# Retention attention with a gated feed-forward on one core: separate attention steps in place of a three-chunk group, and a first part shared out otherwise

## The chip, the core and the metric

The kernel runs on one NeuronCore of a Trainium2 chip. The core has five engines that work side by side, each through its own queue and in order: PE (TensorE, matrix multiplication; its weight loads are listed as PEld), DVE (VectorE), ACT (ScalarE), POOL (GpSimd) and SP (SyncE, which here only issues DMAs). Matrix products go from SBUF to PSUM[...]. The metric is the time of one execution on the device in microseconds (us), less is better.

## The reference

There are q, k and v of shape 8 x 8 x 576 x 64 (batch, heads, sequence, head dimension), all float32. The reference computes retention, which is attention without a softmax, and then a feed-forward layer:

```python
scores = scale * np.matmul(q, k.transpose(0, 1, 3, 2))
Dmat = np.where(rel >= 0, gamma[:, None, None] ** rel[None, :, :], 0.0)   # rel = row - column
attn_out = np.matmul(scores * Dmat, v)
x = attn_out.transpose(0, 2, 1, 3).reshape(B * S, H * D)                  # 4608 x 512
h = x @ w_in                                                            # 4608 x 2048
out = (h * (1.0 / (1.0 + np.exp(-beta * h)))) @ w_out                    # 4608 x 512
```

Each head has its own decay gamma, and beta has a value for each of the 2048 hidden columns.

## The kernel before

**Attention.** A batch's 576 positions are cut into four chunks of 128 and one of 64, so there are 40 chunks, numbered from 0 in order of batch and position; chunks 4, 9, 14 and so on have 64 rows. The decay is taken apart: q is multiplied by a power of gamma that depends on its position, v by the inverse power. So inside a chunk only a causal mask is left, and what earlier chunks contribute is a running sum of k times v, the state. For chunk i there are these steps, whose names are used throughout:

- `pre`: scale and cast q to `qn`, cast k to `kn`, scale and cast v to `vn`. For chunks 0 to 3 this is shared by DVE (qn), ACT (kn) and POOL (vn), later all is POOL's.
- `load_next`: issue the loads of q, k, v seven chunks ahead (`NQ`) on SP.
- `a_T`: eight PE transposes of qn and kn into one PSUM tile `T`, then one ACT copy of it to `qkT` (L193, L197).
- `a_sc`: eight score matmuls. A head has 64 dimensions, so each uses 64 of the 128 array rows (L209). DVE then multiplies by the mask, twice, to give `R` (L213).
- `a_O`: eight matmuls of R with vn (L224). Each takes 64 columns of vn, the two heads of a pair going to the lower and upper 64 partitions of `O`. If the chunk is not the batch's first, four matmuls of q with the state `sbd` are added (L228). DVE copies O to `xT` (L231), the transposed input of the feed-forward layer.
- `a_st`: four matmuls that add the chunk to the state (L243), and two ACT copies to `sbd` (L249). It is left out for a batch's last chunk.

**Feed-forward.** The 4608 tokens are cut into nine blocks of 512. A block m has 16 `up` steps (four matmuls of 512 columns and a Silu on ACT, L261 and L263), then 16 `down` steps (four matmuls each, L273); after every fourth, DVE copies the result to `ot` and SP stores it (L279, L281). Weights are loaded in four pieces each, and cast by DVE and POOL (`cast_w_in`, L124; `cast_w_out`, L136, which divides by beta).

**Order.** The order is written out by hand. `merged` walks through a list of up and down steps, here called fills, and puts attention steps between them at given positions. Until chunk 3 attention runs alone, with matmuls on zeros (`warm_up`, L146) in the gaps. Chunks 4 to 8 are placed as separate steps: `attn_steps(i, at)` puts `pre` four fills ahead, a_T at `at`, a_sc two fills later, a_st and a_O two fills after that. From chunk 9 on `cluster(i, at)` puts three steps of successive chunks in one place:

```python
st += [(at - 4, F(pre, i)), (at - 3.9, F(load_next, i)), (at, F(a_T, i))]
st += [(at, F(a_sc, i - 1))]
st += [(at, F(a_O, i - 2)), (at, F(a_st, i - 2))]
```

The lines are those of the kernel before.

Of the kernel before, what the change touches and what calls it, by code (L numbers as in the profile page):

```python
# [19 lines left out]
def kernel(  # L20
# [10 lines left out]
    nc = tc.nc  # L31
# [51 lines left out]
    for h in range(H):  # L83
# [12 lines left out]
                            fill=0.0, base=0, channel_multiplier=-1)  # L96

    NS = 2
    sbds = [consts.tile([P, HP, P], BF16, name=f"sbd{i}") for i in range(NS)]
    nc.vector.memset(sbds[0][:], 0.0)  # L100
    nc.vector.memset(sbds[1][:], 0.0)

# [6 lines left out]
    WG = 4  # L109
    FG = d_ff // WG  # L110
    w_in_r = moe_w_in.rearrange("(ko ki) f -> ki ko f", ki=P)
    w_out_r = moe_w_out.rearrange("(fo fi) n -> fi fo n", fi=P)
    wts = {}

    def load_w_in(g):
        t = stage.tile([P, KO, FG], F32, name="wt", tag="wt", bufs=4)
        nc.sync.dma_start(t[:], w_in_r[:, :, g * FG:(g + 1) * FG])
        wts[g] = t

    def cast_w_in(g):  # L120
        t = wts.pop(g)
        for ko in range(KO):
            e = nc.gpsimd if ko == KO - 1 else nc.vector
            e.tensor_copy(w_in_sb[:, ko, g * FG:(g + 1) * FG], t[:, ko])  # L124

    def load_w_out(g):
        t = stage.tile([P, KO, d_model], F32, name="wt", tag="wt", bufs=4)
        nc.sync.dma_start(t[:], w_out_r[:, g * KO:(g + 1) * KO, :])
        wts[WG + g] = t

    def cast_w_out(g):
        t = wts.pop(WG + g)
        for i in range(KO):
            fo = g * KO + i
            e = nc.gpsimd if i == KO - 1 else nc.vector
            e.tensor_scalar(w_out_sb[:, fo, :], t[:, i], rbeta_sb[:, fo:fo + 1], None, ALU.mult)  # L136

    for g in range(WG):
        load_w_in(g)
# [8 lines left out]
    def betas():  # L148
        pb = psum.tile([P, FO], F32, name="pb", tag="T", bufs=1)
        nc.tensor.transpose(pb[:], beta_rows[:], ident_f[:FO, :FO])  # L150

        nc.vector.tensor_copy(beta_sb[:], pb[:])
        nc.vector.tensor_tensor(tiny[:], beta_sb[:], beta_sb[:], ALU.mult)  # L153
        nc.vector.tensor_scalar(tiny[:], tiny[:], 1e-24, 1e-12, ALU.is_lt, ALU.mult)
        nc.vector.tensor_tensor(beta_sb[:], beta_sb[:], tiny[:], ALU.add)
        nc.vector.reciprocal(rbeta_sb[:], beta_sb[:])
# [6 lines left out]
    def pre(i):  # L163
# [5 lines left out]
        qn = sb.tile([P, H, D], BF16, name="qn", tag="qn", bufs=3)  # L169
        kn = sb.tile([P, H, D], BF16, name="kn", tag="kn", bufs=4)  # L170
        vn = sb.tile([P, H, D], BF16, name="vn", tag="vn", bufs=4)
        gq_b = gq[:cL, c, :].unsqueeze(2).to_broadcast([cL, H, D])
        gv_b = gv[:cL, c, :].unsqueeze(2).to_broadcast([cL, H, D])
        (nc.vector if first else nc.gpsimd).tensor_tensor(qn[:cL], t[:cL, 0], gq_b, ALU.mult)  # L174
        if first:
            nc.scalar.copy(kn[:cL], t[:cL, 1])
        else:
            nc.gpsimd.tensor_copy(kn[:cL], t[:cL, 1])  # L178
        nc.gpsimd.tensor_tensor(vn[:cL], t[:cL, 2], gv_b, ALU.mult)  # L179
        live[i] = dict(qn=qn, kn=kn, vn=vn)  # L180

# [4 lines left out]
    def a_T(i):  # L186
# [3 lines left out]
        T = psum.tile([P, 2, HP, P], BF16, name="T", tag="T", bufs=1)  # L190
        for j, src in enumerate((L["qn"], L["kn"])):
            for p in range(HP):
                nc.tensor.transpose(T[:, j, p, :cL],  # L193
                                    src[:cL, 2 * p:2 * p + 2, :].rearrange("p h d -> p (h d)"),
                                    ident[:cL, :cL])
        qkT = sb.tile([P, 2, HP, P], BF16, name="qkT", tag="qkT", bufs=4)
        nc.scalar.copy(qkT[:, :, :, :cL], T[:, :, :, :cL])  # L197
        L["qT"], L["kT"] = qkT[:, 0], qkT[:, 1]
# [17 lines left out]
    def a_O(i):  # L216
        b, c = order[i]
        c0, cL = chunks[c]
        L = live[i]
        R, vn = L["R"], L["vn"]  # L220
        O = psum.tile([P, HP, P], F32, name="O", tag="O", bufs=1)
        for p in range(HP):
            for j in range(2):
                nc.tensor.matmul(O[j * D:(j + 1) * D, p, :cL], vn[:cL, 2 * p + j, :], R[:cL, j, p, :cL],  # L224
                                 start=(p == 0), stop=(c == 0), skip_group_check=True)
        if c > 0:
            for p in range(HP):
                nc.tensor.matmul(O[:, p, :cL], sbds[(i - 1) % NS][:, p, :], L["qT"][:, p, :cL],  # L228
                                 start=False, stop=True, skip_group_check=True)
        n0 = b * S + c0  # L230
        nc.vector.tensor_copy(xT[:, :, n0:n0 + cL], O[:, :, :cL])  # L231

    def a_st(i):
# [8 lines left out]
        for p in range(HP):  # L242
            nc.tensor.matmul(st[:, p, :], L["kn"][:cL, 2 * p:2 * p + 2, :].rearrange("p h d -> p (h d)"),  # L243
                             L["vn"][:cL, 2 * p:2 * p + 2, :].rearrange("p h d -> p (h d)"), start=(c == 0 and p == 0), stop=True,
                             skip_group_check=True)
# [55 lines left out]

    warm_up(12)
    betas()
    pre(0)
    a_T(0)
    pre(1)
    for i in range(4):
        warm_up(2)
        a_sc(i)
        a_st(i)  # L310
        if i < 3:
            a_T(i + 1)
            if i < 2:
                pre(i + 2)
        else:
            cast_w_in(0)
            warm_up(2)
        a_O(i)

    fill = [F(up, 0, fo) for fo in range(FO)]  # L320
    merged(fill, [(2, F(cast_w_in, 1)), (5, F(cast_w_in, 2)), (9, F(cast_w_in, 3))],
           [(5.1 + g / 10, F(load_w_out, g)) for g in range(2)],
# [3 lines left out]
    for i in range(5):  # L326
# [18 lines left out]
                                          if b * S + chunks[c][0] + chunks[c][1] >= (m + 1) * MB), len(order)))  # L345

    C0 = done
    clusters = []

    def cluster(i, at):  # L350
        last = len(order) - 1
        st = []
        if i <= last:
            st += [(at - 4, F(pre, i)), (at - 3.9, F(load_next, i)), (at, F(a_T, i))]
        if C0 <= i - 1 <= last:
            st += [(at, F(a_sc, i - 1))]
        if C0 <= i - 2 <= last:
            st += [(at, F(a_O, i - 2)), (at, F(a_st, i - 2))]
        return st

    for m in range(1, NMB - 1):
        base = n1 if m == 1 else len(fill)
        if m > 1:
            fill += [F(up, m, fo) for fo in range(FO)]
            fill += [F(down, m, ms, f0) for ms in range(MB // P) for f0 in range(0, FO, 4)]
        todo = list(range(done, need(m + 1) + 2))
        streams += [cluster(i, base + n * 31 / len(todo)) for n, i in enumerate(todo)]
        done = need(m + 1) + 2
    for m in range(NMB - 1, NMB):
        fill += [F(up, m, fo) for fo in range(FO)]  # L370
        fill += [F(down, m, ms, f0) for ms in range(MB // P) for f0 in range(0, FO, 4)]
    merged(fill, *streams)

# [29 lines left out]
```

## Time and profile before

| | |
|---|---|
| median of three runs | 333.45 us (333.25 to 335.33) |
| the profiled execution | 333.45 us |
| its span, first to last instruction | 331.7 us |
| mean granted TensorE clock | 0.994 |
| PE busy | 318.0 us, 96% of the span |
| ACT, DVE, POOL busy | 165.5, 111.3, 110.3 us |
| read from HBM, written | 36.71 MB, 9.44 MB |

The span is what the profile sees; the time has some 1.75 us more around it. A line of a timeline gives start, duration, engine, source line, operation, output and inputs, shape and count, and in brackets how long the engine was idle before and for whom. Matmuls overlap in the pipeline, so the durations shown for them add up to more than the time that passes: it is the starts that tell the pitch. Some matmul records are missing, so that 7 or 31 stand where 8 or 32 ran.

### The profile page before, as it was taken

How to read it: one execution, taken by the hardware profiler on the slowest of the kernel's cores; microseconds unless marked ns; L12 is line 12 of the kernel's file. 1: busy time of each engine (PE TensorE's matmuls, PEld its weight loads, DVE VectorE, ACT ScalarE, POOL GpSimd, SP SyncE). 2: the span in 40 equal slices, each digit the busy share in tenths (PEclk: the TensorE clock that was granted, in tenths of full speed). 3: DMA queues.
4: the chain of work that ended last, by engine and by line, in shares of the span. 5: the costliest groups of instructions: out<-in, count | busy, mean ns of one | idle time of the engine just before them, and what ended most of it. 6: DMA issues, size and time to landing. Idle time of an engine off the chain costs nothing.

```text
span 331.7 us, 5914 instructions
## 1 busy us (share of the span) xinstructions
PE 318.0 (96%) x2415; PEld 169.1 (51%) x2455; DVE 111.3 (34%) x202; ACT 165.5 (50%) x272; POOL 110.3 (33%) x129
## 2 busy tenths in 40 slices
PE   6779899999999999999999999999999999999995
PEld 2544584576555555555555554555554555444442
DVE  3774372624531244123331232123333332220011
ACT  2667781295337722871188226822784257405700
POOL 2224757975443333322335333323335200000000
PEclk9799999999999999999999999999999999999999
DMA  9999999999999988904692169313000110011011
GB/s 171 220 383 226 268 375 219 209 211 234 243 189 271 209 151 199 196 1 104 154 239 62 40 158 239 74 35 110 34 1 2 63 65 0 2 68 58 2 63 63
DMA packets 121979, 46.53 MB, mean 140 GB/s; under 512 B 113232, under 2 KB 113248, under 8 KB 121952
## 3 DMA queue, kind: packets, MB, share of 16 engines
q1 hardware_dynamic: 121920, 46.15, 62.4%
q8 instruction: 19, 0.31, 0.4%
q14 instruction: 8, 0.07, 0.1%
q10 hardware_dynamic: 32, 0.01, 0.0%
HBM read 36.71 MB, written 9.44 MB: 139 GB/s over the span
## 4 chain that ended last, share of the span: by engine, by line
PE 94%; DVE 3%; issue 1%; ACT 0%
PE ph L261 38%; PE po L273 37%; PE T L193 5%; PE O L224 4%; PE sc L209 4%; PE O L228 3%; PE st L243 2%; PE ph L146 2%; DVE R L213 2%; DVE xT L231 0%; ACT qkT L197 0%; DVE w_in_sb L124 0%; DVE tiny L153 0%; DVE ot L279 0%; DVE qn L174 0%
## 5 line engine op out<-in xcount | busy, mean ns | idle before, releaser
L261 PE MATMUL ph<-xT,w_in_sb 128*128 128x512 bf16 (+2 forms) x622 | 126.9, 357 | 2.2 <-DVE xT L231 1.1
L273 PE MATMUL po<-w_out_sb,gT 128*128 128x512 bf16 x556 | 125.7, 379 | 1.1
L263 ACT ACTIVATE gT<-ph,beta_sb 128x512 bf16<-128x512 f32 (+2 forms) x160 | 102.0, 645 | 39.1 <-PE ph L261 37.9
L261 PEld LDWEIGHTS <-w_in_sb 128*128 128x128 bf16 x640 | 60.5, 98 | 60.0 <-issue 1.6
L273 PEld LDWEIGHTS <-gT 128*128 128x128 bf16 x576 | 55.3, 98 | 63.2
L213 DVE TENSOR_TENSOR R<-sc,causal 128x512 bf16<-128x512 f32 (+1 forms) x80 | 47.2, 631 | 114.6 <-PE sc L209 114.2
L197 ACT COPY qkT<-T 128x1024 bf16<-128x1024 bf16 (+1 forms) x40 | 37.0, 924 | 90.8 <-PE T L193 90.7
L179 POOL TENSOR_TENSOR vn<-qkvn,gv 128x512 bf16<-128x512 f32 (+1 forms) x40 | 41.6, 1040 | 65.9 <-PE st L243 26.7
L279 DVE COPY ot<-po 128x512 f32<-128x512 f32 x36 | 24.8, 691 | 85.4 <-PE po L273 85.4
L178 POOL CAST kn<-qkvn 128x512 bf16<-128x512 f32 (+1 forms) x36 | 21.9, 608 | 70.6 <-PE st L243 53.0
L174 POOL TENSOR_TENSOR qn<-qkvn,gq 128x512 bf16<-128x512 f32 (+1 forms) x36 | 37.6, 1045 | 2.9 <-DMA qkvn<-in_q_dram 2.4
L249 ACT CAST sbd<-st 64x256 bf16<-64x256 f32 x64 | 23.4, 366 | 15.8 <-PE st L243 14.7
L231 DVE CAST xT<-O 128x512 bf16<-128x512 f32 (+1 forms) x40 | 25.3, 632 | 6.0 <-PE O L228 5.5
L224 PE MATMUL O<-R,vn 128*64 128x128 bf16 (+1 forms) x320 | 16.9, 221 | 2.0 <-DVE R L213 2.0
L193 PE MATMUL T<-ident,qn 128*128 128x128 bf16 (+1 forms) x160 | 14.9, 216 | 2.4 <-DVE qn L174 2.4
L193 PEld LDWEIGHTS <-qn 128*128 128x128 bf16 (+1 forms) x160 | 11.1, 98 | 11.6 <-issue 3.0
L209 PE MATMUL sc<-qkT 64*128 64x128 bf16 (+1 forms) x320 | 15.8, 216 | 0.7 <-ACT qkT L197 0.7
L193 PE MATMUL T<-ident,kn 128*128 128x128 bf16 (+1 forms) x160 | 14.9, 216 | 0.0
L224 PEld LDWEIGHTS <-vn 128*64 128x64 bf16 (+1 forms) x320 | 10.6, 109 | 7.3 <-issue 3.9
L209 PEld LDWEIGHTS <-qkT 64*128 64x128 bf16 (+1 forms) x320 | 9.3, 97 | 7.0 <-ACT qkT L197 2.6
L243 PE MATMUL st<-vn,kn 128*128 128x128 bf16 x128 | 12.7, 223 | 0.0
L228 PE MATMUL O<-qkT,sbd 128*128 128x128 bf16 (+1 forms) x128 | 11.9, 215 | 0.0
(37 smaller groups left out, 71.6 us busy)
## 6 DMA issues: line engine op xcount, KB each, us to landing
out_dram<-ot SPq DMA_DIRECT2D x36, 256.0 KB, 2.2
qkvn<-in_q_dram SPq DMA_DIRECT2D x32, 256.0 KB, 4.7
qkvn<-in_k_dram SPq DMA_DIRECT2D x32, 256.0 KB, 5.1
qkvn<-in_v_dram SPq DMA_DIRECT2D x32, 256.0 KB, 5.1
wt<-in_moe_w_in_dram SPq DMA_DIRECT2D x4, 1024.0 KB, 10.3
wt<-in_moe_w_out_dram SPq DMA_DIRECT2D x4, 1024.0 KB, 10.2
qkvn<-in_q_dram SPq DMA_DIRECT2D x8, 128.0 KB, 4.8
qkvn<-in_k_dram SPq DMA_DIRECT2D x8, 128.0 KB, 4.6
```

Of the source, the lines that this page charges most:

```text
L174: (nc.vector if first else nc.gpsimd).tensor_tensor(qn[:cL], t[:cL, 0], gq_b, ALU.mult)
L179: nc.gpsimd.tensor_tensor(vn[:cL], t[:cL, 2], gv_b, ALU.mult)
L193: nc.tensor.transpose(T[:, j, p, :cL], src[:cL, 2 * p:2 * p + 2, :].rearrange("p h d -> p (h d)"), ident[:cL, :cL])
L197: nc.scalar.copy(qkT[:, :, :, :cL], T[:, :, :, :cL])
L209: nc.tensor.matmul(sc[j][:cL, p, :cL], L["kT"][r, p, :cL], L["qT"][r, p, :cL], start=True, stop=True, skip_group_check=True)
L213: nc.vector.tensor_tensor(R[:cL, j, :, :cL], sc[j][:cL, :, :cL], m_b, ALU.mult)
L224: nc.tensor.matmul(O[j * D:(j + 1) * D, p, :cL], vn[:cL, 2 * p + j, :], R[:cL, j, p, :cL], start=(p == 0), stop=(c == 0), skip_group_check ...
L231: nc.vector.tensor_copy(xT[:, :, n0:n0 + cL], O[:, :, :cL])
L261: nc.tensor.matmul(ph[:, :tn], w_in_sb[:, ko, fo * P:(fo + 1) * P], xT[:, ko, x0:x0 + tn], start=(ko == 0), stop=(ko == KO - 1))
L263: nc.scalar.activation(gT[:, fo, t0:t0 + tn], ph[:, :tn], ACT.Silu, scale=beta_sb[:, fo:fo + 1])
L273: nc.tensor.matmul(po[:], gT[:, fo, ms * P:(ms + 1) * P], w_out_sb[:, fo, :], start=(fo == 0), stop=(fo == FO - 1))
L279: nc.vector.tensor_copy(ot, po[:])
```

## The change

1. From chunk 9 on the grouped steps are gone: every chunk has separate steps by `attn_steps`, with the score matmuls two fills after the transposes, and O and the state two fills after these. In block m the chunks are placed that block m + 1 needs, no longer two beyond.
2. v is written by POOL into one of three zeroed tiles `vpads`, of 128 columns for each head: the head's 64 columns in the half that belongs to it, zeros in the other. The matmuls of R with v are then full-width ones that add to all 128 partitions of O. They come after the state matmuls, and all of the first heads of the pairs ahead of the second. `a_st` reads v from the same tile through a strided view.
3. In chunks 0 to 3 the queries' transposes go to `T` and are copied by ACT, while the keys' go to a tile of their own (`T2`, in the PSUM buffers that up and down use) and are copied by DVE. kn is cast by DVE in place of ACT, xT is copied by ACT (chunk 3: half each). Each chunk is finished, O included, ahead of the next one's transposes. `betas` comes after chunk 0, and there are fewer warm-up matmuls in places.
4. The first quarter of the input weights is loaded and cast as two pieces of 256 columns, so there are five pieces.
5. kn, vn and qkT have three buffers (vn's are the vpads) in place of four.

```diff
+    NV = 3
+    vpads = [consts.tile([P, H, P], BF16, name=f"vpad{i}") for i in range(NV)]
...
+    nc.gpsimd.memset(vpads[0][:], 0.0)
     nc.vector.memset(sbds[0][:], 0.0)
+    nc.vector.memset(vpads[1][:], 0.0)
+    nc.vector.memset(vpads[2][:], 0.0)
...
+    pieces = [(0, 256), (256, 256)] + [(f, 512) for f in range(512, d_ff, 512)]
...
-        vn = sb.tile([P, H, D], BF16, name="vn", tag="vn", bufs=4)
+        vp = vpads[i % NV]
+
+        vp4 = vp.rearrange("p (pr two) (x d) -> p pr (two x) d", two=2, x=2)[:, :, 0::3, :]
...
-        if first:
-            nc.scalar.copy(kn[:cL], t[:cL, 1])
-        else:
-            nc.gpsimd.tensor_copy(kn[:cL], t[:cL, 1])
-        nc.gpsimd.tensor_tensor(vn[:cL], t[:cL, 2], gv_b, ALU.mult)
+        (nc.vector if first else nc.gpsimd).tensor_copy(kn[:cL], t[:cL, 1])
+        nc.gpsimd.tensor_tensor(vp4[:cL], t[:cL, 2].rearrange("p (pr two) d -> p pr two d", two=2),
+                                gv_b.rearrange("p (pr two) d -> p pr two d", two=2), ALU.mult)
...
+        T2 = psum.tile([P, 2, HP, P], BF16, name="T2", tag="mm", bufs=3) if i < 4 else T
+        qkT = sb.tile([P, 2, HP, P], BF16, name="qkT", tag="qkT", bufs=3)
+        for j, (src, t) in enumerate(((L["qn"], T), (L["kn"], T2))):
...
+            if i < 4:
+                (nc.vector.tensor_copy if j else nc.scalar.copy)(qkT[:, j, :, :cL], t[:, j, :, :cL])
+        if i >= 4:
+            nc.scalar.copy(qkT[:, :, :, :cL], T[:, :, :, :cL])
...
-        for p in range(HP):
-            for j in range(2):
-                nc.tensor.matmul(O[j * D:(j + 1) * D, p, :cL], vn[:cL, 2 * p + j, :], R[:cL, j, p, :cL],
-                                 start=(p == 0), stop=(c == 0), skip_group_check=True)
+        n = 0
         if c > 0:
             for p in range(HP):
                 nc.tensor.matmul(O[:, p, :cL], sbds[(i - 1) % NS][:, p, :], L["qT"][:, p, :cL],
-                                 start=False, stop=True, skip_group_check=True)
+                                 start=(n == 0), stop=False, skip_group_check=True)
+                n += 1
+        for j in range(2):
+            for p in range(HP):
+                nc.tensor.matmul(O[:, p, :cL], vp[:cL, 2 * p + j, :], R[:cL, j, p, :cL],
+                                 start=(n == 0), stop=(j == 1), skip_group_check=True)
+                n += 1
...
+    warm_up(10)
     pre(0)
     for i in range(4):
+        a_T(i)
         warm_up(2)
         a_sc(i)
+        if i < 3:
+            pre(i + 1)
         a_st(i)
+        warm_up(1 if i else 2)
+        a_O(i)
+        if i == 0:
+            betas()
+        elif i < 3:
             warm_up(2)
+
+    cast_w_in(0)
+    cast_w_in(1)
...
-    for m in range(1, NMB - 1):
-        base = n1 if m == 1 else len(fill)
-        if m > 1:
-            fill += [F(up, m, fo) for fo in range(FO)]
-            fill += [F(down, m, ms, f0) for ms in range(MB // P) for f0 in range(0, FO, 4)]
-        todo = list(range(done, need(m + 1) + 2))
-        streams += [cluster(i, base + n * 31 / len(todo)) for n, i in enumerate(todo)]
-        done = need(m + 1) + 2
-    for m in range(NMB - 1, NMB):
+    todo = list(range(done, need(2)))
+    streams += [attn_steps(i, n1 + n * 30 / len(todo)) for n, i in enumerate(todo)]
+    done = need(2)
+    for m in range(2, NMB):
+        base = len(fill)
         fill += [F(up, m, fo) for fo in range(FO)]
         fill += [F(down, m, ms, f0) for ms in range(MB // P) for f0 in range(0, FO, 4)]
+        if m + 1 < NMB:
+            todo = list(range(done, need(m + 1)))
+            streams += [attn_steps(i, base + n * 31 / len(todo)) for n, i in enumerate(todo)]
+            done = need(m + 1)
```

## The prediction

> **What bounds the kernel now.** I read the page's busy shares first, then PE's own timeline, then the timeline of all engines over the first 50 us.
>
> ```profile
> PE 318.0 (96%) x2415; PEld 169.1 (51%) x2455; DVE 111.3 (34%) x202; ACT 165.5 (50%) x272; POOL 110.3 (33%) x129
> ...
> PE O L224 <- DVE R L213: 2.0, 5, 0.5
> ```
>
> PE is busy for 96% of the span. All its idle time for R is 2.0 us, and the five places lie before 41 us in the timeline. From 49 us on PE waits for nobody, so there the time is the sum of its matmuls, and a change is priced by the pitch from one group of matmuls to the next. (The printed durations overlap, so I use starts.)
>
> First, an attention chunk as separate steps; chunk 7 runs so already (start, us, engine, line, operation, operands, shape, count):
>
> ```profile
> 54.86 0.39 PE L193 MATMUL T<-ident,qn 128*128 128x128 bf16 x4
> 55.08 0.39 PE L193 MATMUL T<-ident,kn 128*128 128x128 bf16 x4
> 55.30 1.89 PE L273 MATMUL po<-w_out_sb,gT 128*128 128x512 bf16 x8
> 57.13 0.40 PE L209 MATMUL sc<-qkT 64*128 64x128 bf16 x8
> 57.46 1.90 PE L273 MATMUL po<-w_out_sb,gT 128*128 128x512 bf16 x7
> 59.20 0.39 PE L243 MATMUL st<-vn,kn 128*128 128x128 bf16 x4
> 59.51 0.41 PE L224 MATMUL O<-R,vn 128*64 128x128 bf16 x8
> 59.86 0.40 PE L228 MATMUL O<-qkT,sbd 128*128 128x128 bf16 x4
> 60.09 0.39 PE L193 MATMUL T<-ident,qn 128*128 128x128 bf16 x4
> ```
>
> Then three chunks' steps in one group, as from chunk 9 on:
>
> ```profile
> 116.43 0.39 PE L193 MATMUL T<-ident,qn 128*128 128x128 bf16 x4
> 116.66 0.39 PE L193 MATMUL T<-ident,kn 128*128 128x128 bf16 x4
> 116.98 0.40 PE L209 MATMUL sc<-qkT 64*128 64x128 bf16 x8
> 117.30 0.41 PE L224 MATMUL O<-R,vn 128*64 128x128 bf16 x8
> 117.65 0.40 PE L228 MATMUL O<-qkT,sbd 128*128 128x128 bf16 x4
> 117.88 0.39 PE L243 MATMUL st<-vn,kn 128*128 128x128 bf16 x4
> ```
>
> Last, what the start waits for:
>
> ```profile
> 23.28 10.52 PE L261 MATMUL ph<-xT,w_in_sb 128*128 128x512 bf16 x47 [0.89 <-DVE xT L231]
> ...
> 42.64 1.71 DVE L136 TENSOR_SCALAR w_out_sb<-wt,rbeta_sb 128x512 bf16<-128x512 f32 x3 [0.87 <-DMA wt<-in_moe_w_out_dram]
> ...
> 44.28 1.27 DVE L213 TENSOR_TENSOR R<-sc,causal 128x512 bf16<-128x512 f32 x2
> ...
> 45.43 0.56 PE L224 MATMUL O<-R,vn 128*64 128x128 bf16 x8
> 45.92 0.40 PE L228 MATMUL O<-qkT,sbd 128*128 128x128 bf16 x4
> ```
>
> The first up matmul starts at 23.28. At 42.64 DVE is waiting for the first output weights; R of chunk 6 stands behind their casts in DVE's queue, and O of chunk 6 behind R. That landing is a clock for PE's start, whatever happened before.
>
> **What the Trainium skill says.** "TensorEngine Tiling (Array Packing)", Key Properties: changing the tiling mode drains the array, and tiles run independently. The trace agrees: sc (64 rows) starts 0.10 after the eight fill matmuls before it end (57.13 - 55.30 - 8 x 0.2158), and O on 64-column halves starts 0.31 after st, against 0.23 for four st matmuls. TensorE's page ("TensorE: Matmul & The Clock Gate", Part 3, The mechanism) has tiles in other column groups run at the same time: partly so, eight half-width O matmuls take 0.35 (59.51 to 59.86, 43 ns each), where full-width ones go at 0.22 for four T (55 to 57 ns each). "DMA: Bandwidth & Descriptors", Why small descriptors are slow, has a fixed cost for each packet: the windows show 219 GB/s at 14 to 16 us (256 B rows of q, k, v) and 388 at 24 to 26 us (2 KB rows of weights).
>
> **The change part by part.**
>
> *Ungrouping, chunks 9 to 39.* A fill matmul takes 0.2158 (64 of the last up phase, 300.15 to 313.96). Before: T of chunk 9 starts at 66.28, the last grouped O ends at 293.24: 226.96 us. In it lie 64 matmuls of 320 columns at 0.136 (24 in 66.62 to 69.89), 8.70, and 800 of 512 columns, 172.64. The rest, 45.6 us, is attention, 1.47 for each of 31 chunks.
>
> After, a full chunk step by step: T 0.44; entry into sc 0.10; sc 0.33; st 0.24; state matmuls 0.23; the eight R matmuls, now 128 columns wide with zeros in half of them, at T's pace, 8 x 0.0565 = 0.45. Sum 1.79. The column halves' 0.09 of mode change goes, their 0.35 becomes 0.45. A first chunk has no state part: 1.56. A 64-row chunk: T enters a 64-row mode, 0.09, and takes 0.34 (66.28 to 66.62); sc 0.10 + 0.25 (from chunk 4); state 0.12; then R with 64-row weights, entry 0.09 and 0.34 as for its T. Sum 1.33.
>
> There are six batches of five (1.56 + 3 x 1.79 + 1.33 = 8.26) and one 64-row chunk more: 50.9. Less 45.6: **+5.3 us**, all on PE, nothing beside it. Chunks 4 to 8, separate already, change by 5 x 0.02 and, for chunk 4, 0.1: +0.2. Bounds: if padded R matmuls went at the halves' 43 ns, 31 x 0.11 = 3.3 less, +2; if each O also paid a mode change of 0.1, +8.
>
> *Do the steps fit without a wait?* Separate steps are two fills (1.73 us) apart. T to sc, in an up phase: ACT ends the running Silu and copies qkT; at 103.38 T started and the copy ran from 104.17 to 105.17, 1.79 after; sc comes at 0.44 + 1.73 = 2.17. Cover 0.38. ACT's two sbd copies (0.76) fall beside the PE time of st and O and are over before the next T, three fills on. R: 0.43 after sc's start, 1.29 long, so 1.72; O's second half is needed at 0.33 + 1.73 + 0.24 + 0.23 = 2.5. Cover 0.8, and an ot copy (0.69) in front fits. So zero; if ACT is late by 0.4 at each of the some 16 up-phase chunks, up to 6 us. POOL has 2.7 us for a chunk (qn 1.04, kn 0.61, vn 1.04) in 7 us, and pre stays four fills ahead: zero, the strided vp write taken as 1.04 too (if doubled, it still fits). The q, k, v loads that pre frees on SP move with it and go seven chunks ahead.
>
> *The start.* qn and kn are cast by DVE, no longer behind betas, qT by ACT and kT by DVE, xT by ACT. POOL's last vn begins at 17.47, upon v's landing, and ends at 18.5; k of chunk 3 lands some 1.2 earlier (spacing of loads), so kn, T, kT and sc end near 18.3, R (1.29) near 19.7, O 20.0, half an xT 20.4, the first cast of a 256-column piece (at most 0.36) 20.8: up from about 21.0, 2.3 earlier. New DVE casts (0.36 to 0.50 by L124's row; kT from PSUM 0.36 to 0.69) make about 3 us a chunk against the loads' 3.6: hidden. The memsets of vpads (POOL at most 8 x 0.22, DVE 2 x 0.54) end before v and q land: hidden. Two first pieces have 1 KB rows: between the two DMA rates, 0 to 0.3 us later for every later weight; I take 0.15.
>
> *What keeps that lead?* Not the loads: their order and bytes are the same, and SP issues without break. T of chunk 4 needs POOL's kn, done at 33.2 after the last input weights' cast; it ran at 33.73, so at most 0.7 is left. At chunk 6, w_out casts end at 44.35 (+0.15), R at 45.55, then the last four R matmuls: 45.85 + 0.15 = 46.0, against 46.15 now, the state part being done first. **-0.15**, and if nothing of DMA is late, -0.3. What is late next is T of chunk 7 with 0.7 of room. The warm-ups only fill waits.
>
> Sum: 5.3 + 0.2 - 0.15 = +5.35. The profiled execution took 333.45 (span 331.7 and 1.75 around it), which is the median of the three too: **338.8 us**.
>
> **The rivals.**
>
> *Half the surcharge:* padded R at 43 ns, or separate sc for nothing. For: half-array matmuls may be held by something other than streaming. Against: T, st and state matmuls of the same width all go at 55 to 58 ns. +2.4: 335.9.
>
> *Waits return:* in up phases sc waits for qkT, since the group had a whole spacing of cover and 0.38 is left. 16 x 0.3 = 5 more, 343.5. Against: chunks 7 and 8 show no wait, though in a down phase.
>
> *Faster:* the 2.3 us at the start survive, because the w_out landing moves forward with the work, or R of chunk 6 gets ahead of it. Place: DVE's queue at 42 us. It decides as soon as the surcharge is under the lead kept; with padded R at 43 ns and the short chunks' 1.0 that is 333.45 - 2.3 + 1.2 = 332.3. Against: DMA is at 1.0 of its share from 38 to 50 us, and DVE's order is unchanged there.
>
> *It doesn't do what it says:* keys' transposes may not overlap queries' copies. Costs some tenths in a start that has 2 us of slack: same number as mine.
>
> **How the numbers follow.** Mine 0.72 (own range 337.0 to 340.3), half 0.13, waits 0.10, faster 0.05. The range leaves out the faster case and most of the waits: 335.8 to 341.0. This kernel can tell about 1%, 3.3 us, from no change: slower 0.83, same 0.12, faster 0.05.
>
> **What would show it.** PE from T to the next T, less fills, 1.8 for a full chunk; O's R group 128 wide, 0.45; first up near 21 and DVE waiting for w_out at 42.6 to 42.9; O of chunk 6 ending near 46; PE's waits in the steady part near zero. I am wrong if the padded O shows under 50 ns each, if sc shows waits on ACT, or if down starts a microsecond earlier.

## The result and the profile after

The kernel after takes 338.92 us (median of four runs, 338.66 to 339.19), the kernel before 333.5 on the same footing. The ratio, taken over all runs and not from the two medians, is 1.015, with a 95% interval of 1.0113 to 1.0188: slower by 1.5%. The profiled execution of after took 338.66 us with a span of 336.9, against 333.45 and 331.7 before; 5.21 us are to be found.

The busy shares first, from the page of after (busy us, share of the span, instructions):

```profile
PE 322.4 (96%) x2420; PEld 173.8 (52%) x2460; DVE 115.6 (34%) x212; ACT 161.3 (48%) x272; POOL 113.0 (34%) x131
```

PE is still the bound. PE's waits in after, from 50 us to the end:

```profile
PE po L299 <- issue: 1.0, 6, 0.2
PE ph L287 <- issue: 0.3, 2, 0.2
```

Each line gives what PE waited for, the total, the number of times and the longest; "issue" means that nothing in the profile shows a reason. No wait on another engine is among them, so the steady part is again a sum of matmuls. (At 119.20 below, such a wait of 0.16 stands where the record of a matmul is missing.) PE's timeline of after, for a full chunk from its transposes to the next chunk's (start, us, engine, line, operation, operands, shape, count):

```profile
116.37 0.39 PE L209 MATMUL T<-ident,qn 128*128 128x128 bf16 x4
116.60 0.39 PE L209 MATMUL T<-ident,kn 128*128 128x128 bf16 x4
116.82 1.89 PE L299 MATMUL po<-w_out_sb,gT 128*128 128x512 bf16 x8
118.64 0.40 PE L227 MATMUL sc<-qkT 64*128 64x128 bf16 x8
119.20 1.67 PE L299 MATMUL po<-w_out_sb,gT 128*128 128x512 bf16 x7 [0.16 <-issue]
120.71 0.39 PE L269 MATMUL st<-vpad,kn 128*128 128x128 bf16 x4
120.93 0.39 PE L243 MATMUL O<-qkT,sbd 128*128 128x128 bf16 x4
121.16 0.61 PE L248 MATMUL O<-R,vpad 128*128 128x128 bf16 x8
121.60 1.89 PE L299 MATMUL po<-w_out_sb,gT 128*128 128x512 bf16 x8
123.33 0.39 PE L209 MATMUL T<-ident,qn 128*128 128x128 bf16 x4
```

Six fill steps, 24 matmuls, lie in it (one is missing from the records, so a 7 stands for 8): 6.96 - 24 x 0.2158 = 1.78 us for the chunk. The padded R matmuls take 121.60 - 121.16 = 0.44.

Last the start, from the timeline of all engines of after:

```profile
21.96 10.73 PE L287 MATMUL ph<-xT,w_in_sb 128*128 128x512 bf16 x47 [0.72 <-DVE w_in_sb L137]
...
33.64 0.29 PE L209 MATMUL T<-ident,kn 64*128 64x64 bf16 x4 [0.27 <-POOL kn L190]
...
42.98 1.71 DVE L149 TENSOR_SCALAR w_out_sb<-wt,rbeta_sb 128x512 bf16<-128x512 f32 x3 [1.42 <-DMA wt<-in_moe_w_out_dram]
...
45.94 0.38 PE L248 MATMUL O<-R,vpad 128*128 128x128 bf16 x4 [0.22 <-DVE R L231]
46.16 2.82 PE L287 MATMUL ph<-xT,w_in_sb 128*128 128x192 bf16 x32
...
54.86 0.39 PE L209 MATMUL T<-ident,qn 128*128 128x128 bf16 x4
```

The first up matmul comes at 21.96, 1.32 earlier than before. By chunk 6 nothing is left of it: DVE waits for the output weights until 42.98 (before: 42.64), the fill after O of chunk 6 starts at 46.16 in both kernels, and T of chunk 7 at 54.86 in both. PE's timeline of before:

```profile
46.16 2.83 PE L261 MATMUL ph<-xT,w_in_sb 128*128 128x192 bf16 x32
...
66.28 0.29 PE L193 MATMUL T<-ident,qn 64*128 64x64 bf16 x4
...
300.15 13.98 PE L261 MATMUL ph<-xT,w_in_sb 128*128 128x512 bf16 x63
```

and of after:

```profile
66.28 0.29 PE L209 MATMUL T<-ident,qn 64*128 64x64 bf16 x4
...
305.34 13.98 PE L287 MATMUL ph<-xT,w_in_sb 128*128 128x512 bf16 x63
```

So the 5.21 us can be placed with two marks, T of chunk 9 and the first matmul of the last up block:

| stretch | before | after | difference |
|---|---|---|---|
| start to T of chunk 9 | 66.28 | 66.28 | 0.00 |
| T of chunk 9 to the first matmul of the last up block | 233.87 | 239.06 | +5.19 |
| from there to the end of the span | 31.55 | 31.56 | +0.01 |

All of it lies where the groups were. The second stretch is called the steady stretch below.

### The profile page after: what moved, and what is told of

Same layout as the page of the kernel before. It is cut to its first block, busy times and chain, and to the rows that moved or that the text cites. A ratio compares the mean times of both kernels' runs of the same rounds, so it can differ in the third digit from the quotient of the medians.

```text
span 336.9 us, 5983 instructions
## 1 busy us (share of the span) xinstructions
PE 322.4 (96%) x2420; PEld 173.8 (52%) x2460; DVE 115.6 (34%) x212; ACT 161.3 (48%) x272; POOL 113.0 (34%) x131
## 4 chain that ended last, share of the span: by engine, by line
PE 84%; DMA 6%; SPq 5%; issue 1%; DVE 1%; ACT 1%; POOL 0%; POOLq 0%
PE po L299 37%; PE ph L287 32%; PE O L248 4%; PE T L209 4%; DMA qkvn<-in_q_dram 4%; SPq L63 4%; PE sc L227 3%; DMA wt<-in_moe_w_out_dram 2%; PE st L269 2%; PE O L243 2%; SPq L129 1%; ACT gT L289 1%; DVE w_out_sb L149 0%; DVE R L231 0%; ACT qkT L215 0%
## 5 line engine op out<-in xcount | busy, mean ns | idle before, releaser
L287 PE MATMUL ph<-xT,w_in_sb 128*128 128x512 bf16 (+2 forms) x623 | 132.6, 357 | 2.2 <-DVE w_in_sb L137 0.7
L299 PE MATMUL po<-w_out_sb,gT 128*128 128x512 bf16 x555 | 130.1, 379 | 1.7 <-issue 1.0
L287 PEld LDWEIGHTS <-w_in_sb 128*128 128x128 bf16 x640 | 58.3, 98 | 55.2 <-DVE w_in_sb L137 1.6
L215 ACT COPY qkT<-T 128x1024 bf16<-128x1024 bf16 (+1 forms) x36 | 32.9, 914 | 65.1 <-PE T L209 65.1
L191 POOL TENSOR_TENSOR vpad<-qkvn,gv 128x512 bf16<-128x512 f32 (+1 forms) x40 | 41.7, 1042 | 30.4 <-DMA qkvn<-in_v_dram 11.6
L256 DVE CAST xT<-O 128x512 bf16<-128x512 f32 (+1 forms) x36 | 22.7, 632 | 37.5 <-PE O L248 37.5
L248 PE MATMUL O<-R,vpad 128*128 128x128 bf16 (+1 forms) x320 | 23.4, 213 | 1.2 <-DVE R L231 1.2
L248 PEld LDWEIGHTS <-vpad 128*128 128x128 bf16 (+1 forms) x320 | 18.2, 97 | 2.5 <-issue 1.8
L269 PE MATMUL st<-vpad,kn 128*128 128x128 bf16 x128 | 12.4, 219 | 2.4 <-POOL vpad L191 2.4
L269 PEld LDWEIGHTS <-kn 128*128 128x128 bf16 x128 | 9.7, 98 | 8.8 <-issue 2.0
```

The lines of the kernel that those rows point to most:

```text
L191: nc.gpsimd.tensor_tensor(vp4[:cL], t[:cL, 2].rearrange("p (pr two) d -> p pr two d", two=2), gv_b.rearrange("p (pr two) d -> p pr two d", ...
L248: nc.tensor.matmul(O[:, p, :cL], vp[:cL, 2 * p + j, :], R[:cL, j, p, :cL], start=(n == 0), stop=(j == 1), skip_group_check=True)
L287: nc.tensor.matmul(ph[:, :tn], w_in_sb[:, ko, fo * P:(fo + 1) * P], xT[:, ko, x0:x0 + tn], start=(ko == 0), stop=(ko == KO - 1))
L299: nc.tensor.matmul(po[:], gT[:, fo, ms * P:(ms + 1) * P], w_out_sb[:, fo, :], start=(fo == 0), stop=(fo == FO - 1))
```

## The experiments

My theory was that of the prediction: separate steps and padded R matmuls cost PE time, each by changes of the array's mode and by R's width, and the early start is lost at the output weights' landing. The rivals were waits on ACT, R matmuls held by something else than their number, and a start that only some detail keeps from counting. The marks of all runs (us):

| run | first up | T of chunk 7 | steady stretch | against before |
|---|---|---|---|---|
| before | 23.28 | 54.86 | 233.87 | |
| after | 21.96 | 54.86 | 239.06 | +5.19 |
| e1_ungroup | 22.53 | 54.82 | 238.42 | +4.55 |
| e2_pad_grouped | 22.92 | 54.95 | 237.62 | +3.75 |
| e3_halves_in_turn | 23.27 | 54.73 | 234.17 | +0.30 |
| e4_start_only | 24.97 | 56.42 | 233.86 | -0.01 |
| e5_lower_twice | 23.55 | 57.16 | 240.01 | +6.14 |
| e6_four_pieces | 23.39 | 54.96 | 239.06 | +5.19 |
| e7_gap3 | 21.01 | 55.67 | 238.92 | +5.05 |
| e8_gates_moved | 21.07 | 56.48 | 239.06 | +5.19 |
| e9_st_between | 23.19 | 54.95 | 236.42 | +2.55 |
| e10_gates_again | 23.49 | 54.82 | 239.06 | +5.19 |

### Ungrouping alone

e1_ungroup is before with the order of after from chunk 9 on; v and R stay as they were.

```diff
-    for m in range(1, NMB - 1):
...
-        streams += [cluster(i, base + n * 31 / len(todo)) for n, i in enumerate(todo)]
...
+    todo = list(range(done, need(2)))
+    streams += [attn_steps(i, n1 + n * 30 / len(todo)) for n, i in enumerate(todo)]
...
+            streams += [attn_steps(i, base + n * 31 / len(todo)) for n, i in enumerate(todo)]
```

> The kernel before, with the separate steps of the changed kernel from chunk 9 on, and nothing else of the change (half-width v, old start). By the sum of matmul pitches: a full chunk 1.78 us as chunks 7 and 8 of before, a first one 1.55, a 64-row one 1.24, so 50.0 for 31 chunks against 45.6: +4.4, about 337.9. If the surcharge is the padded v alone: 333.5. If ungrouping brings waits for qkT or R: 340 or more, with PE waiting for ACT or DVE after 70 us.

Measured: 338.33 us, ratio 1.0133 [1.0098, 1.0168]; the steady stretch +4.55. PE's timeline of e1_ungroup, the last third of a full chunk:

```profile
120.45 0.39 PE L243 MATMUL st<-vn,kn 128*128 128x128 bf16 x4
120.76 0.41 PE L224 MATMUL O<-R,vn 128*64 128x128 bf16 x8
121.11 0.40 PE L228 MATMUL O<-qkT,sbd 128*128 128x128 bf16 x4
121.34 1.89 PE L273 MATMUL po<-w_out_sb,gT 128*128 128x512 bf16 x8
```

From st to the next fill are 0.89 us, as in after (120.71 to 121.60). The half-width R takes 0.35 as in the group, but st ahead of it takes 0.31 where four such matmuls need 0.22: 0.09 to enter the half-width mode. In the group sc stood ahead of R, and sc takes 0.32 to 0.33 whatever follows it (116.98 to 117.30 into R in before's group, 57.13 to 57.46 into a fill), so there the entry added nothing. Ungrouping alone nearly makes the loss.

### Padding alone

e2_pad_grouped is before with the padded v, the state matmuls ahead of R and full-width R matmuls, in the groups of before (four padded tiles, since a group spans more chunks).

```diff
-        vn = sb.tile([P, H, D], BF16, name="vn", tag="vn", bufs=4)
+        vp = vpads[i % NV]
...
-                nc.tensor.matmul(O[j * D:(j + 1) * D, p, :cL], vn[:cL, 2 * p + j, :], R[:cL, j, p, :cL],
-                                 start=(p == 0), stop=(c == 0), skip_group_check=True)
...
+                nc.tensor.matmul(O[:, p, :cL], vp[:cL, 2 * p + j, :], R[:cL, j, p, :cL],
+                                 start=(n == 0), stop=(j == 1), skip_group_check=True)
```

> The kernel before, with the padded v and full-width R matmuls (four padded tiles), groups and start as before. By the sum: each full chunk's eight R matmuls 0.45 in place of 0.35, a 64-row chunk 0.18 more, chunks 4 to 8 0.2 together: +4.0, about 337.5. So each of the two edits alone would cost most of what both cost together (5.4), since with separate steps the halves pay a mode change of 0.09 that padding saves. If padding is free and grouping is all: 333.5. If the two simply add up to 5.4: about 334.5.

Measured: 338.71 us, ratio 1.0153 [1.0106, 1.0199]. Its times reach from 337.39 to 340.43; the profiled one, 337.39, has T of chunk 9 at 66.48 and the steady stretch at +3.75. The median is above what that stretch accounts for, and no profile shows where the longer executions spent it. PE's timeline of e2_pad_grouped, a full group after its transposes:

```profile
118.08 0.40 PE L217 MATMUL sc<-qkT 64*128 64x128 bf16 x8
118.41 0.40 PE L233 MATMUL O<-qkT,sbd 128*128 128x128 bf16 x4
118.65 0.61 PE L238 MATMUL O<-R,vpad 128*128 128x128 bf16 x8
119.09 0.39 PE L254 MATMUL st<-vpad,kn 128*128 128x128 bf16 x4
```

R takes 0.44 in place of 0.35; sc and the state part, now ahead of R, take 0.33 and 0.24, as before to within 0.01. 4.55 and 3.75 make 8.3, but both parts together cost 5.19. The account, chunk by chunk, says why.

### What is in a half-width R

Three edits of before ask why eight R matmuls of half the columns take 0.35. e3_halves_in_turn issues the four lower halves first and the four upper halves after them, so that neighbours in the program no longer lie side by side in the array.

```diff
-        for p in range(HP):
-            for j in range(2):
+        for j in range(2):
+            for p in range(HP):
```

> The kernel before, with the eight half-width R matmuls ordered all lower halves first, then all upper halves, in place of alternating. If the 43 ns of one come from two halves running side by side, they fall back to T's pace, 0.45 for eight: +0.1 for some 32 chunks, +3 to +3.5, about 336.8. If a half-width matmul is short for another reason (a smaller weight load): no change, 333.5.

Measured: 334.09 us, ratio 1.0002 [0.9989, 1.0015]; the steady stretch +0.30. The expectation fell. PE's timeline of e3_halves_in_turn:

```profile
117.27 0.42 PE L224 MATMUL O<-R,vn 128*64 128x128 bf16 x8
117.62 0.40 PE L228 MATMUL O<-qkT,sbd 128*128 128x128 bf16 x4
```

It takes 0.35 as before. Either the halves don't run side by side, or they do whatever their order in the program. The same group in PE's timeline of e3_halves_in_turn, cut off at 117.30, 117.40 and 117.45, shows how many have started by then:

```profile
117.27 0.26 PE L224 MATMUL O<-R,vn 128*64 128x128 bf16 x2
...
117.27 0.31 PE L224 MATMUL O<-R,vn 128*64 128x128 bf16 x4
...
117.27 0.37 PE L224 MATMUL O<-R,vn 128*64 128x128 bf16 x6
```

They start two at a time, 0.05 to 0.06 apart, although four lower halves stand first in the program.

e5_lower_twice puts a price on it. It runs each lower half twice, so the array gets twelve matmuls, eight of them in the lower half. O holds R times v of the first heads twice, so the output is another.

```diff
-                nc.tensor.matmul(O[j * D:(j + 1) * D, p, :cL], vn[:cL, 2 * p + j, :], R[:cL, j, p, :cL],
-                                 start=(p == 0), stop=(c == 0), skip_group_check=True)
+                for again in range(2 - j):
+                    nc.tensor.matmul(O[j * D:(j + 1) * D, p, :cL], vn[:cL, 2 * p + j, :], R[:cL, j, p, :cL],
+                                     start=(p == 0 and again == 0), stop=(c == 0), skip_group_check=True)
```

> The kernel before, with each R matmul of the lower column half done twice and the upper one once, so twelve instead of eight (the first head of each pair counts double in the result). If a lower and an upper half run side by side, the time is that of the longer side, now eight lower ones of 0.056 to 0.065 one after another, 0.45 to 0.52 in place of 0.26: +0.2 for a full chunk, +0.1 for a 64-row one, 6 to 8 us in all, about 340.5. If half-width matmuls just run one after another at some 32 ns each (0.26 for eight, and a mode change), four more cost 0.13: +4 us, about 337.7. If they cost what full-width ones do, 0.22 for four, the count of pairs in the starts would have to be wrong.

Measured: 341.48 us, ratio 1.0215 [1.0195, 1.0234]; the steady stretch +6.14. (Its start also shows 2.3 us more, T of chunk 7 at 57.16; that is not in the stretch.) PE's timeline of e5_lower_twice:

```profile
121.39 0.63 PE L225 MATMUL O<-R,vn 128*64 128x128 bf16 x12
121.95 0.40 PE L229 MATMUL O<-qkT,sbd 128*128 128x128 bf16 x4
```

Four matmuls more take 0.56 - 0.35 = 0.21, or 0.053 each, which is the pitch of a full-width matmul (0.055 to 0.057). One after another, eight halves in 0.35 have at most 0.044 each, and four more would have made at most 0.17, less if the 0.35 holds a change of mode. The distance from 0.21 is small, but with the starts of e3 both say the same: one lower and one upper half go side by side in about the time of one full-width matmul, and a half without a partner takes that time too. Four such slots are 0.21; the other 0.14 of the 0.35 is the change of mode and what lies around it.

The score matmuls, which take half the rows each, go in pairs too. PE's timeline of before, cut off at 117.05 and at 117.16:

```profile
116.98 0.28 PE L209 MATMUL sc<-qkT 64*128 64x128 bf16 x4
...
116.98 0.40 PE L209 MATMUL sc<-qkT 64*128 64x128 bf16 x8
```

All eight have started 0.18 after the first, and R follows at 117.30. So sc too is four slots, 0.22, and about 0.10 for the change of mode behind it.

e9_st_between puts the state matmuls between sc and R in the group, and changes nothing else. R is entered once either way, but from full width and no longer from sc, so the group has four changes of mode in place of three, for each chunk that has a state step.

```diff
-            st += [(at, F(a_O, i - 2)), (at, F(a_st, i - 2))]
+            st += [(at, F(a_st, i - 2)), (at, F(a_O, i - 2))]
```

> The kernel before, with the four full-width state-building matmuls of a group between sc (64 rows) and O (64-column halves) in place of behind O. Nothing is added or taken away, but the array changes its tiling mode four times in a group in place of three. If a mode change has a price of its own, 0.085 to 0.1, the stretch from T of chunk 9 to the last block grows by some 24 groups x 0.09 = 2.1 us, the time to about 335.6. If what separate steps cost comes from something else (waits, order of weight loads): no change.

Measured: 336.25 us, ratio 1.0084 [1.0064, 1.0105]; the steady stretch +2.55. Of the 31 chunks 7 are last of their batch and have no state step: 2.55 / 24 = 0.106 us for one change of mode. PE's timeline of e9_st_between shows where:

```profile
117.60 0.40 PE L209 MATMUL sc<-qkT 64*128 64x128 bf16 x8
117.93 0.40 PE L243 MATMUL st<-vn,kn 128*128 128x128 bf16 x4
118.26 0.41 PE L224 MATMUL O<-R,vn 128*64 128x128 bf16 x8
118.61 0.40 PE L228 MATMUL O<-qkT,sbd 128*128 128x128 bf16 x4
```

st has 0.33 to itself instead of 0.23. The order of matmuls in a group alone is worth 2.5 us.

### The account, chunk by chunk

The four kernels' timelines give the price of each kind of chunk. A batch's five chunks, from the 64-row transposes of chunk 14 to those of chunk 19, less the fills in between: before 89.21 to 123.38 with 124 fill matmuls, e2_pad_grouped 89.81 to 124.59 with 124, e1_ungroup 103.04 to 139.68 with 132, after 103.20 to 139.93 with 132. (The number of fills differs because the order does; each is 0.2158.) A full chunk and a batch's first one are read in the same way from one T to the next; where the next T is a 64-row one, the 0.09 of its entry is taken off (before: 123.38 - 116.43 - 24 x 0.2158 = 1.77, less 0.09). In groups, a full chunk is a group of three full chunks' steps, and a first one a group whose O is a first chunk's. What is left of the batch is the price of the 64-row chunk.

| us | before | padded, in groups (e2) | separate, halves (e1) | both (after) |
|---|---|---|---|---|
| full chunk | 1.68 | 1.78 | 1.78 | 1.78 |
| first chunk | 1.45 | 1.55 | 1.55 | 1.55 |
| 64-row chunk | 0.92 | 1.13 | 1.26 | 1.35 |
| batch: three full, one of each other kind | 7.41 | 8.02 | 8.15 | 8.24 |
| more than before, six batches | | 3.7 | 4.4 | 5.0 |
| measured over the steady stretch | | 3.75 | 4.55 | 5.19 |

The rest, up to 0.2, is the seventh 64-row chunk and the two ends. Two things are read from the table. For a full chunk the two parts don't add: separate halves cost 0.35 and an entry of 0.09, padded ones 0.44, so whichever comes first costs 0.1 and the second nothing. Counting gives the same. A full-width matmul or a pair takes a slot of about 0.056, and a change of mode 0.106 (e9). A full chunk in before is 24 slots (8 for T and 4 each for sc, R, the state part of O, and st) and 3 changes (into sc, from sc to R, out of R); in e1 it is 24 and 4, as R and sc no longer share one; with padding, grouped or not, 28 and 2. That makes 1.66, 1.77 and 1.78 by this estimate, where 1.68, 1.78 and 1.78 were measured. And half of the loss is the single 64-row chunk of each batch: 0.43 of 0.83. In before its transposes share a mode with the scores of the chunk ahead, so that no change lies between them:

```profile
123.51 0.22 PE L193 MATMUL T<-ident,kn 64*128 64x64 bf16 x2
123.55 0.23 PE L209 MATMUL sc<-qkT 64*128 64x128 bf16 x1
123.57 0.22 PE L193 MATMUL T<-ident,kn 64*128 64x64 bf16 x2
123.61 0.40 PE L209 MATMUL sc<-qkT 64*128 64x128 bf16 x7
```

That is PE's timeline of before. The last two transposes and the first score matmul even have their starts in another order than the program's. Alone among the fills, each of these steps has its own entry. Padding takes another part of the 64-row chunk, 0.21 in groups (0.92 to 1.13) and 0.09 on top of separate steps (1.26 to 1.35); no run takes that apart.

### Are there waits to take away?

e7_gap3 is after with three fills between the steps of a chunk in place of two.

```diff
-    streams += [attn_steps(i, n1 + n * 30 / len(todo)) for n, i in enumerate(todo)]
+    streams += [attn_steps(i, n1 + n * 30 / len(todo), 3.0) for n, i in enumerate(todo)]
...
-            streams += [attn_steps(i, base + n * 31 / len(todo)) for n, i in enumerate(todo)]
+            streams += [attn_steps(i, base + n * 31 / len(todo), 3.0) for n, i in enumerate(todo)]
```

> The changed kernel with three fills in place of two between a chunk's separate steps from chunk 9 on. If the steps fit without a wait, as my sum has it: no change, 338.9 within 0.5. If sc waits for qkT or O for R in the up phases, a third fill takes these waits away: 1 to 5 us less.

Measured: 339.05 us, ratio to before 1.0154 [1.0139, 1.0169]; the steady stretch -0.14 against after. PE's waits of e7_gap3 from 60 us on are this one kind:

```profile
PE po L299 <- issue: 0.8, 5, 0.2
```

A third fill of room gains only 0.14, and in neither kernel does PE wait for ACT or DVE here, so such waits are no part of the 5.19. The smaller number of buffers (part 5 of the change) had no run of its own; as PE waits for no engine in this stretch, it shows no cost there.

### The start

e4_start_only has the first four chunks, the pieces of the weights and `betas` of after; v, R and the groups are those of before.

```diff
-        if first:
-            nc.scalar.copy(kn[:cL], t[:cL, 1])
-        else:
-            nc.gpsimd.tensor_copy(kn[:cL], t[:cL, 1])
+        (nc.vector if first else nc.gpsimd).tensor_copy(kn[:cL], t[:cL, 1])
...
+        T2 = psum.tile([P, 2, HP, P], BF16, name="T2", tag="mm", bufs=3) if i < 4 else T
...
+    pieces = [(0, 256), (256, 256)] + [(f, 512) for f in range(512, d_ff, 512)]
```

> The changed kernel's first part alone (first four chunks and five weight pieces), with half-width v and groups as before. My theory: the first up starts 1.3 to 2 us earlier, and nothing of it is left once O of chunk 6 has waited for the casts of the first output weights; 333.2 to 333.6. Rival: the lead survives, 331.2 to 332.2. Rival: the smaller pieces cost, 334.5 or more.

Measured: 334.45 us, ratio 1.0016 [1.0000, 1.0031]; the steady stretch as before. In its profiled execution (334.93) the first up came at 24.97, later than before, and late enough to show: T of chunk 7 started at 56.42, 1.56 later than in before. The timeline of DVE and POOL of e4_start_only shows one reason:

```profile
14.24 1.33 POOL L183 TENSOR_TENSOR vn<-qkvn,gv 128x512 bf16<-128x512 f32 x1 [2.54 <-DMA qkvn<-in_v_dram]
14.59 1.27 DVE L182 CAST kn<-qkvn 128x512 bf16<-128x512 f32 x1
```

The keys' cast on DVE, which the change took from ACT, fell beside POOL's scaling of v and took 1.27. In after's profile the same cast missed it:

```profile
13.06 0.42 DVE L190 CAST kn<-qkvn 128x512 bf16<-128x512 f32 x1
13.91 1.04 POOL L191 TENSOR_TENSOR vpad<-qkvn,gv 128x512 bf16<-128x512 f32 x1 [2.57 <-DMA qkvn<-in_v_dram]
```

There it took 0.42. The Trainium skill ("SBUF — State Buffer", section "SBUF: two separate sides") has DVE and GpSimd share a pair of SBUF ports as an exclusive lock, held for a whole instruction while the other is blocked; on DVE's side it names operations that use both of its port pairs, which casts can, and those with two inputs in SBUF beside a GpSimd one that reads SBUF. The two timelines agree: the slow cast ends at 15.86, 0.29 after POOL's instruction. An operation with two inputs of 16 elements per partition, for betas, took 0.98 beside POOL's vn in e4_start_only and 0.17 alone in after. So the new start has no fixed worth: it depends on how v lands against k.

e6_four_pieces is after with the input weights in four pieces again, which takes away the rows of 1 KB.

```diff
-    pieces = [(0, 256), (256, 256)] + [(f, 512) for f in range(512, d_ff, 512)]
+    pieces = [(f, 512) for f in range(0, d_ff, 512)]
```

> The changed kernel with the input weights in four pieces as before. If the 1 KB rows of the two small pieces are what made v of chunk 3 land at 18.9 and the first output weights 0.3 later, both are back at about 17.5 and 42.6, and the end is at most 0.35 earlier: 338.6. If rows don't matter: 338.9 and the same landings. If the small pieces were worth something: later than 339.2.

Measured: 339.41 us, ratio to before 1.0161 [1.0146, 1.0176]. DVE's first cast of output weights was at 43.06, after's at 42.98, so the 1 KB rows delay nothing that can be seen. T of chunk 7 at 54.96 and the same steady stretch: neither the piece of 256 columns nor the 1.4 us that the first up is later (23.39) shows in the profile. Nor are the 1 KB rows why v of chunk 3 was late in after (below): POOL took it up at 17.42 here, but at 17.37 to 17.50 in e7, e8 and e10 too, which have these rows.

e8_gates_moved asks whether the lead survives if the gates that stand behind POOL's kn and the output weights are moved back by a fill or less.

```diff
-           [(9.5, F(pre, 4)), (12, F(a_T, 4)), (14, F(a_sc, 4)), (16, F(a_O, 4))],
+           [(9.5, F(pre, 4)), (13, F(a_T, 4)), (15, F(a_sc, 4)), (16, F(a_O, 4))],
...
-    streams = [[(4, F(cast_w_out, 0)), (10, F(cast_w_out, 1)), (18, F(cast_w_out, 2)), (21, F(cast_w_out, 3))],
+    streams = [[(4.5, F(cast_w_out, 0)), (10, F(cast_w_out, 1)), (18, F(cast_w_out, 2)), (21, F(cast_w_out, 3))],
```

> The changed kernel, with the casts of the first output weights behind R of chunk 6 in DVE's queue, and transposes and scores of chunk 4 one fill later. If these two are what takes the early start's lead away, T of chunk 7 starts at 54.2 to 54.5 in place of 54.86 (its kn is the next limit) and the end is 0.4 to 0.7 earlier, about 338.4. If the lead is bound elsewhere, T of chunk 7 stays at 54.8 to 54.9. If there was no lead at all, the same.

Measured: 339.85 us, ratio to before 1.0193 [1.0158, 1.0228]; not better. The profiled execution took 342.32, the other three 339.69 to 339.88, so what follows holds for it alone. First up 21.07; R of chunk 6 now got ahead of the output weights' casts in DVE's queue, and the fill after O of chunk 6 started at 45.61, 0.55 earlier than in after. But the transfers were late in this execution: from 38 to 42 us their mean share was 0.56 (0.92 in after), POOL took up the first output weights at 43.96 and DVE, after R, at 44.68. PE's waits of e8_gates_moved show where the lead went:

```profile
PE T L209 <- POOL qn L189: 2.0, 1, 2.0
```

T of chunk 7 waits for POOL's qn and starts at 56.48. POOL had itself been idle for 1.43, waiting for the landing of that chunk's q, whose load is issued behind those of the output weights. POOL's timeline of e8_gates_moved:

```profile
55.06 1.36 POOL L189 TENSOR_TENSOR qn<-qkvn,gq 128x512 bf16<-128x512 f32 x1 [1.43 <-DMA qkvn<-in_q_dram]
```

and, for the same chunk, of after:

```profile
53.28 1.04 POOL L189 TENSOR_TENSOR qn<-qkvn,gq 128x512 bf16<-128x512 f32 x1 [2.06 <-DMA qkvn<-in_q_dram]
54.37 0.61 POOL L190 CAST kn<-qkvn 128x512 bf16<-128x512 f32 x1
```

So there is a second landing behind the first. In after too POOL waited for q, 2.06, and its kn ended at 54.98, 0.11 before the keys' transposes started (55.09). By these times, a lead that got past the output weights could have gained about 0.1 at T of chunk 7 in that execution.

e10_gates_again is the same kernel in another execution.

> A second look at the kernel with the casts of the first output weights behind R of chunk 6. The first look had loads that stood still between 38 and 42 us (0.56 of the DMA engines' time). If that was that execution alone, O of chunk 6 ends near 45.6 again (46.16 in the changed kernel) and T of chunk 7 starts at 54.2 to 54.6. If moving the casts holds the loads up, T of chunk 7 is at 55.5 or later again.

Measured: 338.61 us, the share of the transfers 0.93 from 38 to 42 us, T of chunk 7 at 54.82. But here the keys' cast met POOL's (1.26) and the first up came at 23.49, so there was no lead to keep. Whether a lead would outlast the output weights with these gates moved is not settled: the two executions had either the lead or the timely transfers. The two executions with a first up near 21.0, e7_gap3 and e8_gates_moved, had late output weights (first taken up at 43.52 and 43.96, against 42.98 in after and 42.64 in before). In both, the profiled execution took longer than the kernel's other three. Whether the early start delays the loads or this is chance stays open.

No version came out faster than before; e3_halves_in_turn and e4_start_only equal it within their intervals.

## Why the prediction was right

The forecast was 338.8 us with +5.3, +0.2 and -0.15; the measured median is 338.92, with +5.19 in the steady stretch and 0.00 ahead of it. The large term was right with its reasons. That the total is off by only 0.1 is in part luck: the two small terms were both wrong, of opposite sign, and nearly cancel.

- **Ungrouping, chunks 9 to 39.** Right, and for the reasons given: a full chunk at 1.79 measured 1.78, a first chunk at 1.56 measured 1.55, a 64-row one at 1.33 measured 1.35, and the 1.47 of before is 7.41 / 5 = 1.48. (One slip in its bounds: 31 x 0.11 is 3.4, not 3.3, which changes nothing.) e1 and e2 show that both parts are needed for the whole, and that about half of a batch's loss is the 64-row chunk, which the sum had but did not point out.
- **Half-width R.** The sum 0.35 was right and its split was not. The prediction took 43 ns for each and "partly side by side"; e3_halves_in_turn and e5_lower_twice show pairs, at about 0.053 each, with 0.14 of mode change and what lies around it. The number came out because the trace had given the group's time. For the change it made no difference, but it would have for an edit that adds halves to one side only, as e5 does.
- **Chunks 4 to 8 at +0.2 and the start at -0.15.** Both are 0 within what can be read: T of chunk 7 and of chunk 9 start at 54.86 and 66.28 in both kernels. Separate halves with their entry cost the same 0.44 as padded ones, so the 0.02 per chunk wasn't there. The 0.15 for rows of 1 KB was mis-sized: e6_four_pieces shows no delay.
- **Do the steps fit.** Right. PE's waits show none on ACT or DVE in the steady part, and e7_gap3 gains only 0.14.
- **First up near 21.0.** Reached in two executions (21.01 and 21.07), but 21.96 in after's profile, where v of chunk 3 landed late (POOL took it up at 18.87, in before at 17.47), and 23.4 to 25.0 where DVE's cast met POOL's. The step left out that the two can hold each other up: "qn and kn are cast by DVE, no longer behind betas" took the cast at its price alone.
- **What keeps that lead.** Right as far as O of chunk 6: T of chunk 4 waited 0.40 and 0.27 for POOL's qn and kn, and O of chunk 6 followed the output weights' casts to 46.16, where 46.0 was forecast. Which of the two takes most was not separated. The 0.7 of room at T of chunk 7 was not there in after: its kn was 0.11 ahead. "Not the loads" counted order and bytes, but that chunk's keys land behind the output weights and are a gate of their own.

The rivals fell so. *Half the surcharge*: the padded matmuls go at 0.055, not at 43 ns. *Waits return*: none are there. *It doesn't do what it says*: it does, the keys' transposes of chunk 1 in after (9.55, for 0.40) run beside ACT's copy of the queries (9.64, for 0.59). *Faster*: no run with the new start reached T of chunk 7 more than 0.04 ahead of before (54.82 against 54.86). The way it named, R of chunk 6 ahead of the casts, was made in e8_gates_moved and gained 0.55 there, which the late landing of chunk 7's q took back.

## What to carry to other kernels

Where PE is the bound and waits for nobody, price a reordering from the starts of matmuls, and count the changes of array mode: about 0.1 us each here, so that the order inside a group was worth 2.5 us. Two parts of a change that save or cost the same mode change don't add, and short edge tiles, cheap while they share a mode with a neighbour, can be half of the bill. An earlier start is worth nothing when a landing gates what follows; look for the waits on transfers behind it, one after the other, before counting it.

## What was not expected of the hardware

- One more change of mode cost 0.106 us (2.55 us over 24 chunks). The Trainium skill ("TensorEngine Tiling (Array Packing)", section "Key Properties") says that a change of mode drains the array; the price is from e9_st_between.
- Matmuls on the lower and upper column halves run in pairs even if all lower ones stand first in the program: 0.35 for eight in either order, and 0.21 more for four without a partner.
- Between neighbouring steps of one row mode, starts appear out of program order (a score matmul at 123.55 between transposes at 123.51 and 123.57), and, by the pairs of e3, upper halves start ahead of lower ones. So "in order", as said of the engines at the start, does not hold for PE's matmuls as recorded.
- A cast on DVE took 0.42 alone and 1.26 to 1.27 beside a GpSimd instruction, and whether they met changed from one execution to the next.
